# Four more portions of the second routing phase ahead of the first expert in a fused attention, routing and feed-forward kernel

## The chip, the core and the metric

One core of a Trainium2 chip runs the whole program. TensorE (PE) does matrix products, VectorE (DVE) and ScalarE (ACT) the element-wise work, GpSimd (POOL) and SyncE (SP) start transfers, POOL the gathers among them. Each engine takes its instructions in a fixed order, and they meet by semaphores. The metric is the device time of one execution in microseconds (us), lower is better; the median of several runs counts.

## What is computed

```python
def reference(**kwargs):
    attn_out = _attn_ref(...)                     # (4, 8, 576, 64): banded + downsampled attention
    x = attn_out.transpose(0, 2, 1, 3).reshape(2304, 512)
    x = _moe_ref(x=x, **moe_kwargs)               # 8 experts, each token to one of them
    return _moe2_ref(x=x, **moe2_kwargs)          # dense feed-forward 512 -> 2048 -> 512

def _moe_ref(x, w_gate, w1, w2):
    cap = N // E                                  # 2304 // 8 = 288 rows for each expert
    order = np.argsort(-(x @ w_gate).flatten())
    for idx in order:                             # greedy: the highest logit first
        tok, e = idx // E, idx % E
        if assigned[tok] >= 0 or counts[e] >= cap: continue
        assigned[tok] = e; counts[e] += 1
    for e in range(E):
        out[assigned == e] = np.maximum(x[assigned == e] @ w1[e], 0.0) @ w2[e]

def _moe2_ref(x, w_in, w_out):
    h = x @ w_in
    return (h * np.tanh(softplus(h))) @ w_out
```

## The kernel before

The program has three parts. The attention fills the first 148 us; it leaves the tokens' rows in DRAM (`x_dram`) and the gate's logits in SBUF (`L`). The routed experts run to about 440 us, and the dense feed-forward (groups A to D) after that.

**Routing.** The greedy assignment is done in eight phases; each finds the expert that fills up next and its 288 tokens. `Router.phase(k)` is a generator, and what lies between two of its `yield`s is called a portion here. A phase first makes keys and one-hot rows on DVE. Then come five levels, a search for a threshold digit by digit: DVE compares (`cmp`), PE counts with 18 small matmuls (`cnt`, one more adds the rest that is free), DVE makes a flag (`fl`), PE sums the flags (`j`), DVE reduces them (`jb`) and makes the next `E`. The tail of a phase selects tokens (`sel`), scans them (`run`), has PE place them (`pp`), compares again, and PE and DVE produce the index lists `idx` and `ii` (`it`, `rig`, `ip`) and the number of the expert, `exi`. A last portion issues three gathers of 96 rows each on POOL (`xrow`, L722). Phase 7 has no levels.

**Experts.** `FFN.expert(k, ...)` (E0 to E7) reads the expert's number into a register on SP, fetches eight pieces of weights (`wraw`, 512 KB each, L776), turns the rows over with 12 transposes on PE (`xtp`), and for each of eight `j` makes `hp` (first product), `gh` and `gl` (its two halves after the relu) and, two `j` later, 12 matmuls `ya` (second product). Weights are split by ACT (`wbh`, `wah`) and DVE (`wbl`, `wal`) into two parts. E0 and E2 use the first weights whole ("w"), the others split too ("s"). From the third piece on, E0's weights wait for the last of E0's rows. At an expert's end ACT and DVE split the results (`Yh`, `Yl`) and ACT stores them to `y_dram`.

**Pieces.** `Narrow.piece()` turns 64-bit weights of the dense part into pairs of floats: a load, one ACT operation and six DVE operations on 128 x 512 values (`nz`, `nt`), and a pair that ends it (`wM_sb`). They are put into E0, E2, E5, E6 and E7.

**Order.** `ORDER` says what is written down in which order: `R0` runs the routing until the first gather is out, `H4` four further portions, `E0/1` expert 0 with one piece. An expert has 16 steps, and with each goes one portion of the routing. What an engine's instruction stream is in the end is set by a scheduler that takes this order as priority; `add_manual_dep` with NoSync only holds an order. `busy` (L391) puts constant 128 x 512 matmuls into PE's stream (`idle`), in phase 0 and among the transposes of E0; their result isn't used.

Loads of the dense part's first operands (`Yh`, `Yl` from `y_dram`, L806) are issued early on POOL, between the gathers.

Of the kernel before, what the change touches and what calls it, by code (L numbers as in the profile page):

```python
# [56 lines left out]
class Attn:  # L57
# [175 lines left out]
    def busy(self, n):  # L233

        if not hasattr(self, 'idle'):
            self.idle = self.p_rw.tile([128, 4, 128], F32, name="idle0", tag="rw")
        for _ in range(n):
            m = self.nc.tensor.matmul(self.idle, self.a['fill'], self.a['fill'].unsqueeze(1).to_broadcast([128, 4, 128]), start=True, stop=True)
            if self.mm is not None:
                self.tc.add_manual_dep(m.ins, self.mm.ins.name, mybir.DependencyInfo(mybir.DependencyClass.NoSync, mybir.DependencyReason.DATA), reason="order")  # L240
            self.mm = m
# [95 lines left out]
class Router:  # L337
# [52 lines left out]

    def busy(self, k, n, ins):  # L391

        if k:
            return
        for _ in range(n):
            m = self.nc.tensor.matmul(self.idle.rearrange("p (r n) -> p r n", r=4), self.one, self.one.unsqueeze(1).to_broadcast([128, 4, 128]), start=True, stop=True)
            self.tc.add_manual_dep(m.ins, ins.ins.name, mybir.DependencyInfo(mybir.DependencyClass.NoSync, mybir.DependencyReason.DATA), reason="order")
            ins = m

    def behind(self, ins):  # L400

        if self.mm is not None:
            self.tc.add_manual_dep(ins.ins, self.mm.ins.name, mybir.DependencyInfo(mybir.DependencyClass.NoSync, mybir.DependencyReason.DATA), reason="order")
        return ins

    def phase(self, k):

        nc, wk, sm, L = self.nc, self.wk, self.sm, self.L
# [38 lines left out]
        if not last:  # L447
            for i in range(1, len(SH)):
                if SH[i]:
                    V.tensor_scalar(out=dg[i], in0=key, scalar1=SH[i], scalar2=KS[i] - 1, op0=ALU.arith_shift_right, op1=ALU.bitwise_and)  # L450
                else:
                    V.tensor_scalar(out=dg[i], in0=key, scalar1=KS[i] - 1, scalar2=None, op0=ALU.bitwise_and)
            yield
            for l, K in enumerate(KS):

                if l:
                    cmp = self.compare(E, K, ALU.is_ge, PARTS[k == 0])
                    yield
                end = l == len(KS) - 1
                if not end:  # L460
                    G = sm.tile([128, 18], F32, name="G")
                    V.scalar_tensor_tensor(out=G, in0=E[:, :, 0], scalar=float(KS[l + 1]), in1=dg[l + 1], op0=ALU.mult, op1=ALU.add)

                cnt = self.psr.tile([128, 8], F32, name="cnt", tag="rt")
                nr = lambda a, b: nc.tensor.matmul(cnt, self.one, self.nrem, start=a, stop=b)
                if not k:
                    nr(True, False)
                for c in range(18):
                    if not (l or k) and c == FIRST[0][1]:
                        self.busy(k, 4, ct)  # L470
                    ct = self.behind(nc.tensor.matmul(cnt, cmp[c], OH[:, c], start=(k > 0 and c == 0), stop=(k == 0 and c == 17)))
                if k:
                    nr(False, True)
                self.busy(k, 2, ct)

                fl = sm.tile([128, 8], F16, name="fl")
                V.tensor_scalar(out=fl, in0=cnt, scalar1=0.0, scalar2=None, op0=ALU.is_ge)
                yield
                j8 = self.psr.tile([128, 8], F32, name="j8", tag="rt")
                jm = nc.tensor.matmul(j8, self.sums[:, 128 * l:128 * l + 128], fl, start=True, stop=True)  # L480
                self.busy(k, 7 if end else 4, self.behind(jm))
                jb = sm.tile([128, 1], F32, name="jb")
                V.tensor_reduce(out=jb, in_=j8, op=ALU.max, axis=AX.X)
                if not end:
                    E = P2("E", BF16)
                    V.tensor_scalar(out=E, in0=two(G), scalar1=jb[:, 0:1], scalar2=-1.0, op0=ALU.subtract, op1=ALU.max)

            fw = sm.tile([128, 8], F32, name="fw")
            V.scalar_tensor_tensor(out=fw, in0=j8, scalar=jb[:, 0:1], in1=self.down, op0=ALU.is_ge, op1=ALU.mult)
            fm = sm.tile([128, 1], F32, name="fm")  # L490
            V.tensor_reduce(out=fm, in_=fw, op=ALU.max, axis=AX.X)
            ge = sm.tile([128, 2, 18], F16, name="ge")
            V.tensor_scalar(out=ge[:, 0], in0=E[:, :, 0], scalar1=jb[:, 0:1], scalar2=None, op0=ALU.is_ge)
            V.tensor_scalar(out=ge[:, 1], in0=E[:, :, 0], scalar1=jb[:, 0:1], scalar2=-1.0, op0=ALU.subtract, op1=ALU.is_equal)
        else:
            fw = sm.tile([128, 8], F32, name="fw")
            V.scalar_tensor_tensor(out=fw, in0=self.rem, scalar=30000.0, in1=self.down, op0=ALU.is_lt, op1=ALU.mult)
            fm = sm.tile([128, 1], F32, name="fm")
            V.tensor_reduce(out=fm, in_=fw, op=ALU.max, axis=AX.X)
        n = 18 if last else 36  # L500
# [9 lines left out]
        run = sm.tile([128, 36], F16, name="run")  # L510
# [8 lines left out]
        pp, cn = pc[:, 0:36], pc[:, 36:180]  # L519
        if not last:  # L520
            self.behind(nc.tensor.matmul(cn, self.one, ON.rearrange("p c e -> p (c e)"), start=True, stop=True))
        self.behind(nc.tensor.matmul(pp[:, 0:n], self.tri, s2, start=True, stop=False))
        self.busy(k, 9, nc.tensor.matmul(pp[:, 0:n], self.one, run[:, 0:n], start=False, stop=True))
        V.tensor_scalar(out=full, in0=fw, scalar1=fm[:, 0:1], scalar2=None, op0=ALU.is_equal)
        yield
        pz = sm.tile([128, 36], F32, name="pz")
# [17 lines left out]
        if not last:  # L544
            ct = sm.tile([128, 8], F32, name="ct")
# [4 lines left out]
        it = self.psr.tile([128, 4], F32, name="it", tag="rt")  # L550
        for c in range(18):
            im = self.behind(nc.tensor.matmul(it, oa[c], R[:, c], start=(c == 0), stop=(c == 17)))
        self.busy(k, 28, im)
        ig = self.igw[k % 2]
        li = ig[:, 0:3]
        V.tensor_scalar_add(li, it[0:96, 0:3], 1152.0)
# [110 lines left out]
class FFN:  # L667
# [62 lines left out]
    def expert(self, k, rows, exi):  # L730

        nc, ps = self.nc, self.ps
# [7 lines left out]
        for g in range(3):  # L740
            t = ps['h'].tile([128, 4, 96], F32, name="xtp", tag="h")
            q = slice(96 * g, 96 * g + 96)
            for dc in range(4):
                tp = nc.tensor.transpose(t[:, dc], rows[g][:, 128 * dc:128 * dc + 128], self.a['ident_sb'][0:96, 0:96])
            if g < 2:
                self.busy(k, 1 + g, tp)
            if plain:
                xc = (nc.vector.tensor_copy if g == 1 else nc.scalar.copy)(xh[:, :, q], t)
            else:
                nc.scalar.copy(xh[:, :, q], t)  # L750
                nc.vector.tensor_tensor(out=xl[:, :, q], in0=t, in1=xh[:, :, q].bitcast(F32), op=ALU.subtract)
# [117 lines left out]

ORDER = ('R0 H4 E0/1 E1 E2/2 E3 E4 E5/1 E6/2 E7/2 N A2 A4 A4 A4 A4 B4 B4 B4 B4 B2 C4 C4 C4 C4 C2 D4 D4 D4 D4 D2').split()


MAN = 0
# [33 lines left out]
def body(nc, tc, a):  # L909
    with ExitStack() as ctx:  # L910
# [39 lines left out]
        t0, ng, ns = [0] * 4, 0, 0  # L950
        for st in ORDER:
            st, *pieces = st.split('/')
# [55 lines left out]
```

## Time and profile before

| | |
|---|---|
| median of 3 runs | 851.94 us (849.99 to 852.18) |
| profiled execution | 845.38 us, span 843.6 us |
| PE busy | 812.1 us (96% of the span) |
| DVE busy | 680.3 us (81%) |
| ACT busy | 501.3 us (59%) |
| mean granted clock of TensorE | 0.994 |

The span runs from the first to the last instruction; some 1.8 us lie around it. "Busy" is the time in which an engine works on an instruction. A busy PE is not yet one at its best, since matmuls overlap: where matmuls follow each other closely, their distance counts and not their duration. The granted clock is a share of full speed: 1.00 is 2.4 GHz, 0.50 is 1.2 GHz.

### The profile page before, as it was taken

How to read it: one execution, taken by the hardware profiler on the slowest of the kernel's cores; microseconds unless marked ns; L12 is line 12 of the kernel's file. 1: busy time of each engine (PE TensorE's matmuls, PEld its weight loads, DVE VectorE, ACT ScalarE, POOL GpSimd, SP SyncE). 2: the span in 40 equal slices, each digit the busy share in tenths (PEclk: the TensorE clock that was granted, in tenths of full speed). 3: DMA queues.
4: the chain of work that ended last, by engine and by line, in shares of the span. 5: the costliest groups of instructions: out<-in, count | busy, mean ns of one | idle time of the engine just before them, and what ended most of it. 6: DMA issues, size and time to landing. Idle time of an engine off the chain costs nothing.

```text
span 843.6 us, 16899 instructions
## 1 busy us (share of the span) xinstructions
PE 812.1 (96%) x6236; PEld 685.1 (81%) x6236; DVE 680.3 (81%) x1829; ACT 501.3 (59%) x1209; POOL 175.2 (21%) x215
## 2 busy tenths in 40 slices
PE   8999999889999979899999999999999999999997
PEld 4788877458988979899998888888878888888886
DVE  6999986858889968989958788788888878657664
ACT  4787876023433434446637677777777777765552
POOL 5655320112011011021001000012223211322223
PEclk9999999999999989999999999999999999999999
DMA  8858622256467584478424444457697674973512
GB/s 217 213 169 227 195 87 96 94 178 229 141 220 248 177 269 169 144 281 276 151 97 140 128 135 148 151 160 194 145 231 173 176 194 112 246 167 118 132 51 76
DMA packets 65107, 142.41 MB, mean 169 GB/s; under 512 B 7968, under 2 KB 20640, under 8 KB 65024
## 3 DMA queue, kind: packets, MB, share of 16 engines
q1 hardware_dynamic: 24704, 70.54, 26.7%
q0 software_dynamic: 29280, 56.63, 25.9%
q10 hardware_dynamic: 11040, 14.16, 4.8%
q8 instruction: 49, 0.80, 0.4%
q14 instruction: 34, 0.28, 0.1%
HBM read 112.98 MB, written 18.88 MB: 156 GB/s over the span
## 4 chain that ended last, share of the span: by engine, by line
PE 58%; issue 6%; DMA 4%; POOL 2%; DVE 1%; ACT 1%; POOLq 0%; DVEq 0%
PE hm L704 7%; PE hm L706 7%; PE hm L705 7%; PE oa L705 6%; PE oa L706 6%; PE oa L704 6%; PE ya L704 3%; DMA xrow<-x_dram,idx 3%; PE ya L706 3%; PE ya L705 3%; PE hp L704 2%; PE hp L705 2%; PE hp L706 2%; PE hp L784 2%; DMA Yh<-y_dram 1%
## 5 line engine op out<-in xcount | busy, mean ns | idle before, releaser
L704 PE MATMUL hm<-Yh,wM_sb 128*128 128x512 f32 (+1 forms) x320 | 118.4, 370 | 1.5 <-DMA Yh<-y_dram 1.5
L706 PE MATMUL hm<-Yh,wM_sb 128*128 128x512 f32 (+1 forms) x320 | 118.7, 371 | 0.0
L705 PE MATMUL hm<-Yl,wM_sb 128*128 128x512 f32 (+1 forms) x320 | 118.6, 371 | 0.0
L704 PE MATMUL oa<-wM_sb,gh 128*128 128x512 f32 x288 | 113.1, 393 | 0.0
L705 PE MATMUL oa<-wM_sb,gh 128*128 128x512 f32 x288 | 113.1, 393 | 0.0
L706 PE MATMUL oa<-wM_sb,gl 128*128 128x512 f32 x288 | 112.9, 392 | 0.0
L858 DVE SCALAR_TENSOR_TENSOR eu<-eu 128x512 f32<-128x512 f32 x72 | 49.7, 690 | 45.0 <-ACT eu L857 44.7
L696 ACT CAST wbh<-wraw 128x512 fp32r<-128x512 f32 x64 | 39.8, 622 | 69.1 <-PE ya L705 40.4
L704 PE MATMUL ya<-gh,wbh 128*128 128x288 f32 x256 | 79.5, 314 | 0.0
L706 PE MATMUL ya<-gh,wbl 128*128 128x288 f32 x256 | 77.1, 302 | 0.0
L705 PE MATMUL ya<-gl,wbh 128*128 128x288 f32 x256 | 76.9, 301 | 0.0
L864 ACT CAST gh<-eu 128x512 fp32r<-128x512 f32 x72 | 44.3, 616 | 53.8 <-DVE eu L861 53.5
L704 PEld LDWEIGHTS hm<-Yh,wM_sb 128*128 128x128 f32 x320 | 60.2, 188 | 13.0 <-DMA Yh<-y_dram 1.9
L865 DVE TENSOR_TENSOR gl<-eu,gh 128x512 fp32r<-128x512 f32 x72 | 49.5, 688 | 24.9 <-ACT gh L864 24.4
L705 PEld LDWEIGHTS hm<-Yl,wM_sb 128*128 128x128 f32 x320 | 60.2, 188 | 11.2
L722 POOL DMA_INDIRECT xrow<-x_dram,idx x24 | 30.7, 1280 | 185.9 <-PE ip L564 95.4
L706 PEld LDWEIGHTS hm<-Yh,wM_sb 128*128 128x128 f32 x320 | 60.2, 188 | 10.7
L853 ACT ACTIVATE eu<-hm 128x512 f32<-128x512 f32 x72 | 42.9, 595 | 41.1 <-PE hm L706 40.9
L704 PEld LDWEIGHTS oa<-wM_sb,gh 128*128 128x128 f32 x288 | 54.0, 188 | 12.8 <-ACT osb L829 0.5
L855 ACT ACTIVATE eu<-eu,one_sb 128x512 f32<-128x512 f32 x72 | 52.1, 724 | 20.6 <-DVE eu L854 19.8
L706 PEld LDWEIGHTS oa<-wM_sb,gl 128*128 128x128 f32 x288 | 54.0, 188 | 12.4
L705 PEld LDWEIGHTS oa<-wM_sb,gh 128*128 128x128 f32 x288 | 54.0, 188 | 11.9
(185 smaller groups left out, 2140.8 us busy)
## 6 DMA issues: line engine op xcount, KB each, us to landing
wraw<-in_wE_dram SPq DMA_DIRECT2D x64, 512.0 KB
n<-in_wM_dram SPq DMA_DIRECT2D x32, 512.0 KB
Yh<-y_dram POOLq DMA_DIRECT2D x16, 1024.0 KB, 9.2
Yl<-y_dram POOLq DMA_DIRECT2D x16, 1024.0 KB, 7.1
part<-osb POOLq DMA_DIRECT2D x36, 256.0 KB, 4.3
vw<-in_vw_dram SPq DMA_DIRECT2D x16, 315.0 KB
kT<-in_kT_dram SPq DMA_DIRECT2D x16, 291.0 KB
qT<-in_qT_dram SPq DMA_DIRECT2D x16, 288.0 KB
```

The costliest lines, as they stand in the source:

```text
L696: c = self.nc.scalar.copy(wh, src)
L704: mm(out, lh, rh, start=first, stop=False)
L705: mm(out, lh, rl, start=False, stop=False)
L706: return mm(out, ll, rh, start=False, stop=last)
L722: ld = nc.gpsimd.indirect_dma_start(out=xr, out_offset=None, in_=self.a['x_dram'], in_offset=bass.IndirectOffsetOnAxis(ap=idx[:, g:g + 1], ...
L784: self.r.mm = nc.tensor.matmul(hp, w1[:, 128 * dc:128 * dc + 128], xh[:, dc], start=dc == 0, stop=dc == 3)
L853: nc.scalar.activation(out=e, in_=hp[:, 0:w], func=AF.Exp)
L855: nc.scalar.activation(out=u, in_=e, func=AF.Square, bias=one)
L858: nc.vector.scalar_tensor_tensor(out=u, in0=u, scalar=1.0, in1=r, op0=ALU.add, op1=ALU.mult)
L864: self.cast = nc.scalar.copy(gh[:, 0:w], e)
L865: self.mark = nc.vector.tensor_tensor(out=gl[:, 0:w], in0=e, in1=gh[:, 0:w].bitcast(F32), op=ALU.subtract)
```

## The change

`H4` becomes `H8`: four more portions of phase 1 are written down ahead of E0. The constant matmuls are dealt anew. Behind the index matmuls of phase 0 there are 14 instead of 28. The first level of phase 1 gets 3 behind its counts and 8 behind its flag sum, and E0's first transpose is held behind the last of these eight. Those among the transposes of E0 stay.

```diff
     def busy(self, k, n, ins):
 
-        if k:
+        if k > 1:
             return
         for _ in range(n):
             m = self.nc.tensor.matmul(self.idle...)
             self.tc.add_manual_dep(...)
             ins = m
+        return ins
...
                 if k:
                     nr(False, True)
-                self.busy(k, 2, ct)
+                if k == 0 or (k == 1 and l == 0):
+                    self.busy(k, 2 + k, ct)
...
                 jm = nc.tensor.matmul(j8, self.sums[:, 128 * l:128 * l + 128], fl, start=True, stop=True)
-                self.busy(k, 7 if end else 4, self.behind(jm))
+                self.behind(jm)
+                if k == 0:
+                    self.busy(k, 7 if end else 4, jm)
+                elif k == 1 and l == 0:
+                    self.ready = self.busy(k, 8, jm)
...
-        self.busy(k, 9, nc.tensor.matmul(pp[:, 0:n], self.one, run[:, 0:n], start=False, stop=True))
+        pm = nc.tensor.matmul(pp[:, 0:n], self.one, run[:, 0:n], start=False, stop=True)
+        if k == 0:
+            self.busy(k, 9, pm)
...
-        self.busy(k, 28, im)
+        if k == 0:
+            self.busy(k, 14, im)
...
                 tp = nc.tensor.transpose(t[:, dc], rows[g][:, 128 * dc:128 * dc + 128], self.a['ident_sb'][0:96, 0:96])
-            if g < 2:
+                if k == g == dc == 0:
+                    self.tc.add_manual_dep(tp.ins, self.r.ready.ins.name, ...)
+            if k == 0 and g < 2:
                 self.busy(k, 1 + g, tp)
...
-ORDER = ('R0 H4 E0/1 E1 E2/2 E3 ...').split()
+ORDER = ('R0 H8 E0/1 E1 E2/2 E3 ...').split()
```

The streams change in many places, from E0 to E7. Three of them follow. PE at the start of E0, before (`ip` is the last index matmul of phase 0, `cnt` and `j` belong to phase 1, `hp` is E0's first product; of the counts and constant matmuls only the first rows of a run are shown):

```order
L564 MATMUL ip<-ident_sb,rig_69 72x96
L744 MATMUL xtp<-ident_sb,xrow 128x96 x4
L396 MATMUL idle<-ones_66 128x512
L471 MATMUL cnt<-rOH,cmp 128x8
...
L465 MATMUL cnt<-rnrem,ones_66 128x8
L744 MATMUL xtp<-ident_sb,xrow 128x96 x4
L480 LDWEIGHTS rsum
...
L744 MATMUL xtp<-ident_sb,xrow 128x96 x4
L784 MATMUL hp<-xh,wraw 128x288 x3
```

and now:

```order
L573 MATMUL ip<-ident_sb,rig_69 72x96
L472 MATMUL cnt<-rOH,cmp 128x8
...
L482 LDWEIGHTS rsum
...
L753 MATMUL xtp<-ident_sb,xrow 128x96 x2
L472 LDWEIGHTS cmp
...
L466 MATMUL cnt<-rnrem,ones_66 128x8
L753 MATMUL xtp<-ident_sb,xrow 128x96 x2
...
L753 MATMUL xtp<-ident_sb,xrow 128x96 x4
...
L753 MATMUL xtp<-ident_sb,xrow 128x96 x4
L795 MATMUL hp<-xh,wraw 128x288
```

The counts and the flag sum of phase 1's first level have moved ahead of all transposes, those of its second level in between the first tile's four.

POOL's transfers behind the attention, before (`xrow` x6 are the gathers of two experts, `Yh` and `Yl` the early loads):

```order
L722 DMA xrow<-x_dram,idx 96x512 x6
L806 DMA Yh<-y_dram 128x4x256
L806 DMA Yl<-y_dram 128x4x256
L722 DMA xrow<-x_dram,idx 96x512 x6
L806 DMA Yh<-y_dram 128x4x512
L806 DMA Yl<-y_dram 128x4x512
L722 DMA xrow<-x_dram,idx 96x512 x12
```

and now:

```order
L731 DMA xrow<-x_dram,idx 96x512 x6
L817 DMA Yh<-y_dram 128x4x256
L731 DMA xrow<-x_dram,idx 96x512 x3
L817 DMA Yl<-y_dram 128x4x256
L731 DMA xrow<-x_dram,idx 96x512 x6
L817 DMA Yh<-y_dram 128x4x512
L817 DMA Yl<-y_dram 128x4x512
L731 DMA xrow<-x_dram,idx 96x512 x9
```

The two large loads stood ahead of the gathers of E4 and stand behind them now; one of the smaller ones stands behind the gathers of E2.

DVE at the tail of phase 6, in E5, before:

```order
L659 TENSOR_SCALAR nz<-nt 128x512
L508 SCALAR_TENSOR_TENSOR sel<-raid,fm,sel 128x18
L660 SCALAR_TENSOR_TENSOR nz<-n_4714,nz 128x512
L511 SCALAR_TENSOR_TENSOR run<-ones_66,sel 128x36
L699 TENSOR_TENSOR wbl<-wraw,wbh 128x512
L661 TENSOR_TENSOR nt<-nt,nz 128x512
L794 SCALAR_TENSOR_TENSOR gl<-hp,gh 128x288
```

and now:

```order
L513 SCALAR_TENSOR_TENSOR sel<-own,fm,ge 128x36
L532 TENSOR_SCALAR full<-fw,fm 128x8
L514 SCALAR_TENSOR_TENSOR sel<-raid,fm,sel 128x18
L805 SCALAR_TENSOR_TENSOR gl<-hp,gh 128x288
L517 SCALAR_TENSOR_TENSOR run<-ones_66,sel 128x36
```

The piece's operations have left this tail; they stand further on in the stream, between the `ii` of phase 6 and the `run` of phase 7.

## Rows read from the trace of the kernel before

**Rows 1.** Waits of PE: line, what for, us in total, times, longest

```profile
PE xtp L744 <- DMA xrow<-x_dram,idx: 6.0, 3, 4.9
PE cnt L471 <- DVE cmp L388: 3.2, 8, 1.3
```

**Rows 2.** Windows E0, E1, E2, E4, E5, E6: busy by engine, clock, DMA, GB/s

```profile
175.00:208.00 33.00, 29.84 (x257) 24.57 (x257) 24.30 (x92) 10.30 (x20) 4.68 (x3) 1.00 0.65 232
208.00:241.00 33.00, 32.63 (x354) 31.23 (x352) 28.15 (x104) 13.86 (x29) 5.28 (x5) 1.00 0.63 189
241.00:275.00 34.00, 32.97 (x286) 28.06 (x284) 30.05 (x107) 13.16 (x27) 3.44 (x3) 1.00 0.63 210
307.00:346.00 39.00, 34.05 (x349) 32.80 (x346) 28.88 (x104) 15.17 (x32) 3.01 (x3) 0.91 0.56 173
346.00:377.00 31.00, 28.78 (x251) 27.65 (x251) 28.23 (x104) 14.36 (x31) 4.46 (x3) 0.94 0.58 197
...
390.00:400.00 10.00, 10.00 (x78) 10.00 (x76) 9.89 (x20) 5.88 (x13) 0.00 (x0) 1.00 0.97 327
```

**Rows 3.** The same view, of the stretches behind the holes of E4 and E5

```profile
312.90:318.00 5.10, 5.07 (x36) 4.90 (x37) 1.78 (x4) 1.49 (x4) 0.00 (x0) 0.56 0.02 6
358.30:362.00 3.70, 3.67 (x15) 3.61 (x16) 3.70 (x18) 0.00 (x0) 0.00 (x0) 0.54 0.83 280
```

**Rows 4.** Timeline of PE, start of E4: start, us, instruction [idle before <-releaser]

```profile
312.93 0.90 PE L744 MATMUL xtp<-ident_sb,xrow 96*128 96x96 f32 x4 [4.95 <-DMA xrow<-x_dram,idx]
```

**Rows 5.** Timeline of POOL, 222 to 300 us

```profile
223.79 0.82 POOL L806 DMA_DIRECT2D Yh<-y_dram  x1 [19.27 <-PE j L480]
...
231.62 1.15 POOL L722 DMA_INDIRECT xrow<-x_dram,idx  x1 [5.84 <-PE hp L706]
...
290.87 0.80 POOL L806 DMA_DIRECT2D Yh<-y_dram  x1 [21.45 <-DMA y_dram<-Yl]
...
296.05 1.28 POOL L722 DMA_INDIRECT xrow<-x_dram,idx  x1 [2.82 <-PE ip L564]
```

**Rows 6.** The view of the tile xrow, all gathers

```profile
DMA to landing us min/median/max: 3.0/6.2/16.8
```

**Rows 7.** Timeline of PE, end of phase 0 and start of E0

```profile
165.11 6.20 PE L396 MATMUL idle<-ones 128*128 128x512 f16 x28
...
173.91 0.55 PE L744 MATMUL xtp<-ident_sb,xrow 96*128 96x96 f32 x4
175.03 1.72 PE L784 MATMUL hp<-xh,wraw 128*128 128x288 f32 x6 [0.57 <-ACT xh L748]
...
179.22 0.17 PE L480 MATMUL j<-fl,rsum 128*128 128x8 f16 x1 [1.41 <-DVE fl L477]
...
183.33 0.60 PE L471 MATMUL cnt<-rOH,cmp 128*128 128x8 f16 x18 [1.35 <-DVE cmp L388]
```

**Rows 8.** Timelines of DVE and ACT in the same stretch

```profile
166.64 1.34 DVE L388 TENSOR_TENSOR cmp<-E,rthr 128x2304 f16<-128x2304 bf16 x1
...
177.75 0.62 ACT L696 CAST wbh<-wraw 128x512 fp32r<-128x512 f32 x1 [2.77 <-DMA wraw<-in_wE_dram]
...
178.40 0.69 DVE L699 TENSOR_TENSOR wbl<-wraw,wbh 128x512 fp32r<-128x512 f32 x1 [2.63 <-ACT wbh L696]
...
180.41 0.62 ACT L696 CAST wbh<-wraw 128x512 fp32r<-128x512 f32 x1 [2.05 <-DMA wraw<-in_wE_dram]
```

**Rows 9.** Timeline of DVE in E5, the tail of phase 6

```profile
355.40 0.42 DVE L659 TENSOR_SCALAR nz<-nt 128x512 int32<-128x512 int32 x1
355.74 0.23 DVE L508 SCALAR_TENSOR_TENSOR sel<-raid,fm,sel 128x18 f16<-128x18 f32 x1
355.89 0.69 DVE L660 SCALAR_TENSOR_TENSOR nz<-n,nz 128x512 f32<-128x512 uint32 x1
356.49 0.23 DVE L511 TENSOR_TENSOR_SCAN run<-ones,sel 128x36 f16<-128x36 f16 x1
...
358.32 1.54 DVE L767 TENSOR_TENSOR Yl<-ya,Yh 128x288 fp32r<-128x288 f32 x4
```

More of the change, by code (lines that the diff above doesn't have):

```diff
@@ L744, in expert @@
                 tp = nc.tensor.transpose(t[:, dc], rows[g][:, 128 * dc:128 * dc + 128], self.a['ident_sb'][0:96, 0:96])
-            if g < 2:
+                if k == g == dc == 0:
+                    self.tc.add_manual_dep(tp.ins, self.r.ready.ins.name, mybir.DependencyInfo(mybir.DependencyClass.NoSync, mybir.DependencyReason.DATA), reason="order")
+            if k == 0 and g < 2:
                 self.busy(k, 1 + g, tp)
@@ L868, in group @@
             yield
-ORDER = ('R0 H4 E0/1 E1 E2/2 E3 E4 E5/1 E6/2 E7/2 N A2 A4 A4 A4 A4 B4 B4 B4 B4 B2 C4 C4 C4 C4 C2 D4 D4 D4 D4 D2').split()
+ORDER = ('R0 H8 E0/1 E1 E2/2 E3 E4 E5/1 E6/2 E7/2 N A2 A4 A4 A4 A4 B4 B4 B4 B4 B2 C4 C4 C4 C4 C2 D4 D4 D4 D4 D2').split()
 MAN = 0
```

## The prediction

> **What bounds the kernel now.** The waits of TensorE (PE) come first [rows 1]. In the middle of the program, where the experts run, its waits are few: 6.0 us for gathered rows (4.9 of it once) and 3.2 us for compares of the routing. The second view cuts the experts' part into their stretches [rows 2]: PE is busy 32.63 of 33 us in E1 and 32.97 of 34 in E2, so a gain can only come from the holes, and these are 3.16 us in E0 (33.00 - 29.84), 0.37 in E1, 1.03 in E2, 4.95 in E4 and 2.22 in E5. VectorE (DVE) is busy 24 to 30 us of the same stretches: it isn't the bound, but it has little room. The third view is the clock [rows 3]: behind the holes of E4 and E5 TensorE was granted 0.56 and 0.54 of full speed, that is mostly its lower level (1.2 GHz), over 5.10 and 3.70 us. That costs 5.10 x 0.44 = 2.24 us and 3.70 x 0.46 = 1.70 us more. E4's hole is therefore worth 4.95 + 2.24 = 7.2 us, E5's 2.22 + 1.70 = 3.9 us. After E0's holes of 1.41 and 1.35 us the clock stayed at 1.00 [rows 2].
>
> Whose fault is E4's hole? Its first transpose waits 4.95 us for rows, until 312.93 [rows 4]. The gather was issued at 296.05, behind the two loads of Yh and Yl (1 MB each) that stand from 290.87 on in the same queue [rows 5]. Gathers take 6.2 us to land in the median and 16.8 at most [rows 6]; 312.93 - 296.05 is 16.9, so 16.8 is this one, the first rows being asked for 12 us before they were needed.
>
> **The change part by part.** The sum is made against the profiled execution: 845.38 us, of which 843.6 are its span. The median of the runs shown is 851.94, so I carry differences over.
>
> 1. *Four portions earlier, E4.* Every routing phase now stands four portions further ahead of its expert. One portion goes with each of an expert's 16 steps, and an expert takes 31 to 34 us [rows 2]: by steps that is some 8 us. Read from the order it is less: of the hundred or so DVE rows between the last xl of E3 and the first of E4, the cast that makes the indices of phase 4 is the 60th before and the 41st now, a fifth of some 32 us, so about 6 us. The gather of E4 then goes out at about 290, and in POOL's queue the two 1 MB loads now stand behind it, not ahead. It is needed at 308. Even with the worst landing of the trace (16.8) it would be 307, with the median one 296. I take the whole hole as gone: -7.2 us. The bounds are -7.2 and 0 (rows as late as before).
>
>  What stands behind POOL's new order: the gather of E2 is now queued behind the load of Yh that waits for E0's output (223.79 [rows 5]). The gather would be ready about 6 us before 231.62, at 225.6, so POOL is free again in time; this costs nothing, and if E0's output came 10 us later, E2 would still have its rows. The loads of Yh and Yl that go back are wanted only after E7.
>
>  The Trainium skill, "DMA: Bandwidth & Descriptors", section "Queues, rings and completion order", says that each engine takes the descriptors of one ring in order and goes round-robin between queues. By that rule rows queued behind 2 MB in their own queue come late whatever the other queues do; the trace's 16.8 us agrees. It would put the sum at the same -7.2.
>
> 2. *E2 and E1.* E2's first transposes wait 1.03 us for rows [rows 2]; these were asked for at 231.62 [rows 5] and are now asked for 6 us earlier: -1.0 (bounds -1.0 and 0). The small holes about the start of E1 (0.40 of E0's 3.16 after its two big ones, and 0.37) hang on E1's weights, whose fetch needs the expert's number from the same phase: -0.7 (bounds -0.7 and 0).
>
> 3. *The start of E0.* This is what the change pays. PE's queue now holds the first level and half of the second of phase 1 in front of and among the transposes. The 28 constant matmuls took 6.20 us from 165.11 [rows 7], 0.22 each; 14 end at 168.2. The compare of the first level ends at 167.98 [rows 8], so its 18 counts follow with no wait, to 169.2. DVE has then two splits, a flag, a reduction, a new E and the second level's compare of 1.34 us [rows 8] to do, and is through at about 172.3. PE fills 1.7 of it with 8 constant matmuls; then two transposes, the counts of level two (0.6 us), two transposes, the four of the second tile, the four of the third. The third tile's transposes, which started at 173.91 when their rows had come, now start at about 174.4, and the first matmul of E0, at 175.03 [rows 7], at about 175.5: +0.5. Bounds 0 (rows later than 174.4 anyway) and +1.2 (a second compare's length late).
>
>  Then E0's two holes. Before, a flag of the routing stood in DVE behind a split of weights that landed at 177.75 (cast 177.75, split 178.40 [rows 8]); PE stood 1.41 us in front of the flag's matmul at 179.22, and 1.35 us at 183.33 for a compare held by the weights of 180.41 [rows 7, 8]. The new order of DVE has the same pattern one level on: the flag of level three behind the split of 178.40, the compare of level four behind the split of the weights of 180.41. PE reaches them at 177.8 and 181.0 and is let go at 179.3 and 182.6: 1.5 + 1.6 = 3.1 us against 2.76, +0.3. The weights themselves come no earlier, since their fetch waits for the last of the first rows as before. Together E0 costs +0.8; bounds 0 and +2.
>
>  A rule speaks against this part: the Trainium skill, "TensorE: Matmul & The Clock Gate", section "What happens when you issue a matmul", says that matmuls stay in program order and only weight loads are pulled ahead. The row at 179.22 agrees: ready matmuls stood 1.41 us behind the routing's. If the transposes could pass, the +0.5 would be 0 and the sum 8.2 instead of 7.7.
>
> 4. *E5.* Here PE waited for the tail of phase 6 while DVE worked on a piece of the later weights (nz, nt): 0.42 and 0.69 us between a selection and the run that PE needed [rows 9]. The tail of phase 6 is now free of pieces. But the piece has gone into the tail of phase 7: from the cast of ii to the run of phase 7 the new order of DVE has six such operations (3 x 0.34 + 3 x 0.60 start to start, as 355.40 to 355.74 and 355.89 to 356.49 show [rows 9]), three Yl (1.54 / 4 = 0.38 each [rows 9]) and small ones, 4.9 us, while PE has 21 matmuls of 0.13 us (10.00 / 78 [rows 2]), 2.8 us. So PE stands for about 2.5 us at that run, against 2.22: the hole moves, and I take the clock's loss to come with it, +0.4. Bounds -3.9 (gone) and +1.
>
> 5. *The constant matmuls.* 28 become 14, and 11 come in with phase 1's first level: 3 fewer of 0.22 us, all while the rows are on their way. Nothing, as long as PE has no long gap there; the longest in the new order is under 1 us.
>
> Sum: -7.2 - 1.0 - 0.7 + 0.8 + 0.4 = -7.7 us. 845.38 becomes 837.7, and the median 851.94 - 7.7 = **844.2 us**.
>
> **The rivals.** (a) E5's hole goes too, since DVE runs ahead of where the walk has it: -3.9 - 0.4 more, 839.9. For it: DVE gains some room when E4's hole no longer bunches its work. Against: 2.8 us of PE work against 4.9 us of DVE work. (b) E4's rows still come late, because the weights of E4, asked for earlier too, crowd the same engines: half the wait and the whole loss of clock stay, 2.5 + 2.2 = 4.7, 848.9. Against it: 12 us of margin by the median landing. (c) A new hole of E5's size opens where the routing now meets other DVE work, +3.9: 848.1. DVE at 30.05 of 34 us in E2 [rows 2], whose two pieces now meet the tail of phase 3, speaks for it; that PE has more matmuls between the marks there than in E5 speaks against it. (d) Slower: in E0 the two holes now lie 1.7 us apart instead of 2.7, and TensorE falls to its lower level there. From 177.8 to some 200 every matmul would take twice its time, half of 22 us: +11, 855.2. It decides from where the two holes act like one: the trace has full clock after 1.41 and 1.35 us lying 2.7 us apart, and the lower one after E5's hole, which is shorter than their sum. (e) The portions don't pay: phase 1 hangs on E0's weights, so the later phases gain only a few us and E4's rows stay where they are; only the small terms remain, 850.5.
>
> **How the numbers follow.** Chances: the forecast 0.52 (its own range 842 to 846.5), (a) 0.13, (b) 0.10, (c) 0.12, (d) 0.07, (e) 0.06. A measurement of this kernel can tell about 0.3% from no change, 2.6 us. Faster by more: the forecast, (a), half of (b) and most of (c), 0.80. Within: the rest of (b) and (c), and (e), 0.13. Slower: (d), 0.07. The range for 8 in 10 takes in (b) and (c) and most of (a): 839 to 850.
>
> **What would show it.** In the trace after: no wait of E4's first transpose over 1 us and full clock behind it; the gather of E4 issued about 290 and ahead of the 1 MB loads; E0's first matmul at about 175.5, with two holes of some 1.5 us; E5 with a hole of 2 to 3 us at the run of phase 7 and the lower clock behind it. The prediction is wrong in its main step if the rows of E4 are late again, and wrong in its pay-back if E0 loses more than 2 us or its clock.

## The result: 837.5 us where 844.2 were forecast

| us | before | changed |
|---|---|---|
| median, first comparison (19 executions each) | 851.94 | 837.52 |
| ratio, with its 95% interval | | 0.983 (0.980 to 0.985) |
| ratio in three later comparisons | | 0.987 (0.982 to 0.992), 0.983 (0.979 to 0.987), 0.988 (0.985 to 0.991) |
| median of the executions whose clock is on record (61 and 33) | 850.67 | 837.52 |
| median granted clock of these | 0.988 | 0.996 |
| median of time x granted clock | 840.4 | 833.2 |

The sign was right and the gain nearly twice as large as forecast: 13 to 14 us instead of 7.7, below the low end of the range (839). The last two lines of the table split it: about 7 us are waits, and about 6 us are clock. (Time x clock counts the lower clock also where PE waits anyway, so it is a rough split.) The ratios and the last three lines leave out the few slow executions, which run some 1.5% or more above the fastest at a lower clock.

The profile recorded with the result is of an execution that ran with the lower clock for some 24 us in the attention; the rows below are from another execution of the same kernel (new8_again). Its page has PE busy 97% of a span of 835.4 us:

```profile
span 835.4 us, 16916 instructions
PE 808.7 (97%) x6233; PEld 682.7 (82%) x6233; DVE 679.6 (81%) x1829; ACT 500.7 (60%) x1209; POOL 175.9 (21%) x215
```

The waits of PE, which answer to [rows 1] (line, what for, us in total, times, longest). The wait for rows that headed that list is gone altogether; those for compares, flags and Yl are left:

```profile
PE cnt L472 <- DVE cmp L388: 2.7, 7, 1.1
PE j L482 <- DVE fl L479: 1.6, 2, 1.4
...
PE ya L713 <- DVE Yl L778: 1.2, 2, 1.0
...
PE cnt L472 <- DVE ii L575: 0.9, 1, 0.9
```

The stretches of E0, E1, E2, E4 and E5, which answer to [rows 2] (us, busy time of each engine with its instructions, granted clock, DMA share, GB/s):

```profile
177.00:212.00 35.00, 32.30 (x296) 26.32 (x296) 25.75 (x98) 10.51 (x20) 4.41 (x3) 0.95 0.68 225
212.00:241.00 29.00, 28.96 (x298) 27.82 (x296) 25.20 (x93) 12.66 (x27) 5.47 (x5) 1.00 0.70 213
241.00:277.00 36.00, 36.00 (x315) 31.38 (x313) 33.57 (x115) 14.28 (x30) 2.77 (x3) 1.00 0.65 221
308.00:340.00 32.00, 32.00 (x351) 30.86 (x350) 29.37 (x106) 15.42 (x32) 3.81 (x3) 1.00 0.63 206
340.00:372.00 32.00, 29.91 (x268) 28.24 (x267) 30.31 (x107) 15.63 (x33) 8.51 (x6) 1.00 0.63 209
```

E1, E2 and E4 have no hole at all. E0 has 2.7 us and now a clock of 0.95; E5 has 2.1 us, with full clock.

POOL's timeline, which answers to [rows 5]: the gathers of E4 are asked for at 290.88, and the two loads go out behind them.

```profile
290.88 1.83 POOL L731 DMA_INDIRECT xrow<-x_dram,idx  x1 [28.75 <-PE ip L573]
293.02 0.91 POOL L731 DMA_INDIRECT xrow<-x_dram,idx  x1 [0.30 <-issue]
294.23 1.15 POOL L731 DMA_INDIRECT xrow<-x_dram,idx  x1 [0.30 <-issue]
296.35 0.80 POOL L817 DMA_DIRECT2D Yh<-y_dram  x1 [0.97 <-DMA y_dram<-Yh]
```

And PE at the start of E4, which answers to [rows 4]; seven transposes run with no wait in front of them:

```profile
307.94 0.74 PE L753 MATMUL xtp<-ident_sb,xrow 96*128 96x96 f32 x7
```

**Where the time went, by stage.** The stretches below are cut at the first transposes of the experts in PE's timeline. They begin at the cast of the first list of indices (`idx` of phase 0, in DVE's timeline), since all streams are the same in both kernels up to the end of phase 0, and end at the first `hm`, where the dense part begins. "Five" is the mean over five profiled executions of each kernel.

| us | before, first profile | before, five | changed, five | difference of the fives | forecast |
|---|---|---|---|---|---|
| idx to E1 (with E0) | 43.41 | 42.92 | 45.24 | +2.3 | +0.8 |
| E1 and E2 | 66.69 | 69.11 | 64.52 | -4.6 | -1.7 |
| E3 and E4 | 70.02 | 70.51 | 62.99 | -7.5 | -7.2 |
| E5 | 34.28 | 34.27 | 32.55 | -1.7 | +0.4 |
| E6 and E7 | 56.63 | 56.64 | 56.51 | -0.1 | 0 |
| sum | 271.03 | 273.46 | 261.82 | -11.6 | -7.7 |

The sum lay between 271.0 and 276.9 us in the five executions of before, and between 259.0 and 264.7 in those of the changed kernel; the dense part took 406.5 to 407.2 us in all ten. So 11.6 of the 13 to 14 us are where they were looked for, and three of the terms had the wrong size, one of them the wrong sign.

### The profile page after: what moved, and what is told of

Same layout as the page of the kernel before. It is cut to its first block, busy times and chain, and to the rows that moved or that the text cites. A ratio compares the mean times of both kernels' runs of the same rounds, so it can differ in the third digit from the quotient of the medians.

```text
span 844.8 us, 16916 instructions
## 1 busy us (share of the span) xinstructions
PE 816.6 (97%) x6233; PEld 688.6 (82%) x6233; DVE 681.0 (81%) x1829; ACT 500.9 (59%) x1209; POOL 175.7 (21%) x215
## 3 DMA queue, kind: packets, MB, share of 16 engines
q0 software_dynamic: 29280, 56.63, 26.1%
## 4 chain that ended last, share of the span: by engine, by line
PE 75%; DVE 9%; issue 6%; DMA 5%; POOL 2%; ACT 2%; SPq 0%; POOLq 0%; ACTq 0%; DVEq 0%
PE hm L713 7%; PE hm L715 7%; PE hm L714 7%; PE oa L714 6%; PE oa L715 6%; PE oa L713 6%; PE ya L714 4%; PE ya L715 4%; PE ya L713 4%; PE hp L713 3%; PE hp L795 3%; PE hp L714 3%; PE hp L715 3%; PE cnt L472 2%; PE pvl L223 2%
## 5 line engine op out<-in xcount | busy, mean ns | idle before, releaser
L713 PEld LDWEIGHTS hm<-Yh,wM_sb 128*128 128x128 f32 x320 | 60.3, 188 | 13.2 <-DMA Yh<-y_dram 2.1
L714 PEld LDWEIGHTS oa<-wM_sb,gh 128*128 128x128 f32 x288 | 54.1, 188 | 11.9
```

Source lines behind the costliest of these rows:

```text
L713: mm(out, lh, rh, start=first, stop=False)
L714: mm(out, lh, rl, start=False, stop=False)
```

## The experiments

**The kernel before again** (no edit), for a second profile:

> The kernel before, unchanged, so that its median of 851.94 us has a second profile beside the one of 845.38 us. Theory 1: the 6.6 us between the two lie in the routed experts: in most runs the rows of E4 come still later than in the run first profiled, so a new profile near the median shows a wait of E4's first transpose of 8 to 12 us instead of 4.95, and the lower clock behind it for longer than 5 us. Theory 2: they lie in the attention or in the dense part (clock, loads), and E4's wait is again 4 to 6 us; the changed kernel then gets its additional 6 us from there. Time by both: 849 to 853 us.

849.91 us, and a profile at 849.55. E4's transposes wait 3.37 us (theory 1 had 8 to 12), but E1's wait for rows too, which they did not in the first profile, and the lower clock follows. Neither theory was quite it. Three further profiles of the same kernel followed, to see which of its holes cost clock, and one of the changed kernel:

> A further profile of the kernel before, for how often each of its holes costs clock. Theory (the first profile was one of the best executions, since fewer of its holes drew the lower clock): E4's wait for rows of 3 to 5 us and its loss of 2.5 to 3.4 us of clock are in each of these looks; E1's wait for rows, 1.5 us or more, with 1.7 us of clock, in most of them, and E5's loss of 1.7 us in some; together 5 to 9 us of clock lost between the routing and the dense part. Rival (the executions differ in the attention): the experts lose about 5 us in each, and the attention 0 to 5.

> The same kernel and the same expectation as the look before it.

> The same kernel and the same expectation as the two looks before it.

> A further profile of the changed kernel. Theory: no wait for rows in any expert, 0 to 3.4 us of clock lost in E0 and none in E1 to E7. Rival: E0 loses 3.4 us or more each time that its two holes lie close, and the stretch from the first index cast to the dense part's first matmul is 264 us or more.

The changed kernel had had a second profile before that:

> The changed kernel, unchanged, for a profile without the low clock in the attention (21 to 63 us) that its first profile has. 836 to 838 us; from the casting of the first indices to the first transpose of E7 222 us as in the first profile (231 in the kernel before), E4 without a wait for rows, and a clock of 1.00 through all experts.

The three further executions of the kernel before: 851.84, 851.61 and 849.62 us. The changed kernel: 839.86 us (median, ratio 0.987) and 835.62. In the profile of the first of these E0 takes 41.48 us from its first transpose to E1's and draws the lower clock, so that it is 234.8 us from the cast to E7's first transpose; the first profiles of the two kernels have 241.1 and 232.1 (the 231 and 222 us of the expectation are each 10 us too low). The second takes 261.93 us from the cast to the dense part. In the second of the three further profiles (b_look2) PE's timeline has waits for rows at the starts of E1, E2 and E4 (start, us, instruction, idle before and its releaser), and the pair of waits in E5:

```profile
211.00 0.55 PE L744 MATMUL xtp<-ident_sb,xrow 96*128 96x96 f32 x4 [1.14 <-DMA xrow<-x_dram,idx]
212.05 0.90 PE L744 MATMUL xtp<-ident_sb,xrow 96*128 96x96 f32 x4 [0.50 <-DMA xrow<-x_dram,idx]
...
245.91 0.84 PE L744 MATMUL xtp<-ident_sb,xrow 96*128 96x96 f32 x4 [0.72 <-DMA xrow<-x_dram,idx]
...
316.38 0.55 PE L744 MATMUL xtp<-ident_sb,xrow 96*128 96x96 f32 x4 [3.45 <-DMA xrow<-x_dram,idx]
...
362.80 0.18 PE L523 MATMUL pp<-run,ones 128*128 128x36 f16 x1 [0.57 <-DVE run L511]
364.36 0.41 PE L704 MATMUL hp<-xh,wah 128*128 128x288 f32 x1 [1.38 <-DVE gl L794]
```

Behind each of them the clock fell, as the windows of 5 us of the same execution show (granted clock third from the right):

```profile
210.00:215.00 5.00, 3.50 (x18) 3.31 (x19) 3.04 (x7) 1.33 (x3) 0.00 (x0) 0.69 0.04 10
...
245.00:250.00 5.00, 4.28 (x18) 3.50 (x17) 3.11 (x8) 0.48 (x1) 0.00 (x0) 0.66 0.46 172
315.00:320.00 5.00, 2.67 (x15) 2.19 (x16) 1.81 (x4) 1.42 (x3) 0.00 (x0) 0.77 0.17 48
320.00:325.00 5.00, 5.00 (x41) 4.85 (x40) 1.41 (x4) 1.03 (x3) 0.00 (x0) 0.55 0.02 3
365.00:370.00 5.00, 5.00 (x27) 5.00 (x28) 4.44 (x20) 0.62 (x1) 0.00 (x0) 0.66 0.57 211
```

5 x (1 - 0.69) = 1.6 us, 1.7, then 1.2 + 2.3, then 1.7. Summed over windows of 5 us from the routing to the dense part, the kernel before loses 5.1, 5.2, 6.9, 8.5 and 5.1 us of clock in its five executions, the changed one 0, 1.7, 0, 1.7 and 1.7. E4's hole draws the lower clock in five of five executions, E5's pair of waits in four, E1's rows in two, E2's in one. The attention loses 0, 3.4, 5.2, 1.7 and 3.4 us besides: the first profile is the only one of the five without a loss there. The theory of these runs holds in its main part (the experts lose 5 to 8.5), but E1's clock fell in two of the four and not in most, and the attention has a share, which the change doesn't touch.

**The two loads behind E4's gathers, in the kernel before** (all other engines keep their order):

```diff
-            if k == 0:
-                self.g0 = ld
+            if k in (0, 4):
+                setattr(self, f'g{k}', ld)
...
-            nc.gpsimd.dma_start(t, self.a['y_dram'][...])
+            yl = nc.gpsimd.dma_start(t, self.a['y_dram'][...]); ng = t0 == 2 and part == 0 and self.tc.add_manual_dep(yl.ins, self.g4.ins.name, ...)
```

> The kernel before, with one edit: the two 1 MB loads of Yh and Yl that stand ahead of E4's gathers in POOL's order stand behind them. PE, DVE, ACT and SP keep their order. Theory 1 (most of the change is E4's rows, and the typical run loses more there than the profiled one): 851.9 - 7 to 13, so 839 to 845 us, E4's first transpose with no wait over 1 us and full clock behind it. Theory 2 (the typical run loses elsewhere): no more than the 7.2 us of the profile, 844.5 to 846 us. Rival (the rows are late because of the weights that are under way, not because of these two loads): 850 to 852 us, the wait stays.

841.99 us, ratio 0.989 (0.985 to 0.993). The gathers of E4 are asked for no earlier than before, at 299.54, and the loads follow them:

```profile
299.54 0.91 POOL L722 DMA_INDIRECT xrow<-x_dram,idx  x1 [26.49 <-PE ip L564]
...
303.63 0.83 POOL L806 DMA_DIRECT2D Yh<-y_dram  x1
```

PE's timeline of the same execution, at the start of E4:

```profile
311.81 1.19 PE L744 MATMUL xtp<-ident_sb,xrow 96*128 96x96 f32 x12
```

Twelve transposes run in a row with no wait, 12.3 us after the rows were asked for; behind the loads the same rows took 16.9 us in the first profile and 15.8 in b_look2 (316.38 - 300.58). The stretch of E3 and E4 is 63.99 us, against 70.51: that is 6.5 of the 7.5 us that the change takes off it. The weights that were under way are the same, so the rival falls: the loads ahead in the queue made the rows late. E1's wait for rows is still there in this run (1.60 and 0.66 us, and a clock of 0.77), as nothing was done for it.

**Six portions, constant matmuls as before** (`R0 H6` in the kernel before):

> Six portions ahead of E0, the constant matmuls as before the change. In POOL's order E4's gathers stand behind the 1 MB loads as before the change, but are asked for some 4 us earlier. Theory (E4's rows are late for the loads ahead of them in the queue): a wait for E4's rows of up to 2 us is left, and E1's rows come with less or no wait; 840 to 846 us. If only the time of asking counts and not the place in the queue: no wait in E4, 837 to 840. If only the place counts: the whole wait of 3 to 5 us is there, 845 to 849.

840.19 us, ratio 0.989 (0.985 to 0.993). E4 has no wait. Its gathers stand behind one of the two loads, not behind both as was expected, and are asked for at 290.36, 15.3 us before they are needed (POOL's timeline, then PE's at the start of E4):

```profile
288.21 0.79 POOL L806 DMA_DIRECT2D Yh<-y_dram  x1 [22.78 <-issue]
290.36 1.21 POOL L722 DMA_INDIRECT xrow<-x_dram,idx  x1 [1.35 <-DVE ii L566]
...
294.81 0.82 POOL L806 DMA_DIRECT2D Yl<-y_dram  x1
```

```profile
305.68 0.25 PE L744 MATMUL xtp<-ident_sb,xrow 96*128 96x96 f32 x1
```

How long the three gathers of E4 take from asking to landing goes with what stands ahead of them (the view of the tile `xrow` over these three gathers, first before the change with both loads ahead, then here with one, then in the changed kernel with none):

```profile
DMA to landing us min/median/max: 14.8/16.0/16.8
DMA to landing us min/median/max: 11.2/12.1/12.2
DMA to landing us min/median/max: 6.9/7.1/7.6
```

So each of the two loads ahead goes with some 4 to 5 us. Two remedies were enough: no load ahead with 12.3 us of time, or one load ahead with 15.3. Since six portions moved one load back as well, no run shows what asking earlier is worth with both loads still ahead. The changed kernel has 17.1 us (from 290.88 to 307.94) and no load ahead, which is more margin than needed. E5's hole is not helped by six portions: 1.89 us in one piece, and 3.4 us of clock.

**The dealing alone** (the changed kernel with `R0 H4`), **and the portions alone** (the kernel before with `R0 H8`), the latter three times and twice beside the changed kernel:

> The changed kernel with four portions ahead of E0 instead of eight: the new dealing of the constant matmuls alone. By the prediction it is worth nothing: 850.5 to 853.5 us, with E4's rows late as before (the 1 MB loads stand ahead of its gathers again). If the dealing is itself a part of the gain, it comes out at 846 us or less, E0 starting 2 to 3 us earlier, as 14 constant matmuls of 0.22 us are gone there.

> The kernel before with eight portions ahead of E0 instead of four and nothing else: the portions alone, the constant matmuls as before (28 behind the index matmuls, none with phase 1's first level). By the prediction the dealing is worth nothing, so 837 to 840 us, as the changed kernel. If the dealing pays for the earlier portions' cost, it is slower than the changed kernel: 28 constant matmuls of 0.22 us ahead of phase 1's counts hold these by 3 us, the first product comes 2 to 3 us later, 840 to 843 us.

> Eight portions ahead of E0 with the constant matmuls as before the change, a second time and beside the changed kernel, in five rounds. Theory (the new dealing has a price in E0: its first two holes and sometimes the clock): the stretch from the first index cast to the dense part's first matmul is 259 to 261 us against 262 to 265 with the new dealing, and the median 1 to 4 us below the changed kernel's. Rival (the two profiles differed by chance): the medians agree within 1 us and the stretches overlap.

> The changed kernel beside the one with the dealing as before: 836 to 840 us, E0 39 to 41.5 us from its first transpose to E1's; by the rival of the run above 37 to 38.

> Eight portions with the constant matmuls dealt as before the change. Theory (the new dealing costs E0 some 3 us, as four profiles of the changed kernel beside two of this one have it): E1's first transpose 41 to 43 us after the first index cast, the median 2 to 4 us below the changed kernel's of the same job. Rival (the price is made up for elsewhere, or the profiles were chance): the median within 1.5 us of the changed kernel's, or above it as in the last pair.

> The changed kernel beside it. Theory: E1's first transpose 45 to 48 us after the first index cast, 836 to 840 us. Rival: 42 to 43 us, as in one profile of five.

The dealing alone: 852.75 us, ratio 1.002 (0.999 to 1.005), no gain. The portions alone: 839.74, 838.59 and 838.18 us, with the changed kernel at 835.24 and 838.73 beside the last two. Taken together the medians are 838.28 (15 executions) and 837.52 (33). In the profiles the dealing isn't free: E1's first transpose comes 42.80, 41.35 and 43.11 us after the first index cast with the old dealing and 45.55, 47.70, 42.54, 45.45 and 44.98 with the new one. Of these 2.8 us in the mean, 1.0 is clock: it fell in E0 in three of the five with the new dealing and in none of the three with the old. The profile of the dealing alone has it too (a wait of 3.25 us for a compare, 3.4 us of clock, E1's first transpose after 45.51 us). The times do not show the 2.8 us: the pairs differ by 3.4 us for the new dealing and by 0.6 against it. Where they come back isn't settled, the theory that the new dealing makes the kernel slower is borne out by neither pair, and "the dealing is worth nothing" stands within some 3 us.

**E0's weights earlier** (the dependence "rows first" on the first gather instead of the last, in the changed kernel):

```diff
-            if k == 0:
+            if k == 0 and g == 0:
                 self.g0 = ld
```

> The changed kernel, with E0's weights from the third piece on waiting for the first of E0's three gathers instead of the last. It measures E0's pay-back. Theory (E0's holes of 1.1 to 2.6 us are the routing's flag and compare standing in DVE behind a split whose weights land late): the third piece lands 1.5 to 3 us earlier, the holes shrink by as much each, E0 gets 2.5 to 4 us shorter, and the clock stays at 1.00 in it; 834 to 837 us beside 838 to 840 for the changed kernel. Rival (the weights only change places with the rows): the third tile's transposes wait 1.5 to 2.5 us for rows instead, the first product starts that much later, and the time stays within 1 us of the changed kernel's.

838.40 us, ratio 0.985 (0.977 to 0.994): no gain to be seen. The rival is right. The two holes are gone, and the third tile's rows are late instead, with the lower clock behind it (PE's timeline, then the window):

```profile
175.16 0.90 PE L753 MATMUL xtp<-ident_sb,xrow 96*128 96x96 f32 x4 [1.84 <-DMA xrow<-x_dram,idx]
```

```profile
175.00:180.00 5.00, 4.27 (x29) 3.08 (x30) 1.80 (x4) 2.23 (x4) 0.00 (x0) 0.50 1.03 406
```

Rows and weights share the same 406 GB/s there (DMA share 1.03): this order of the transfers moves the price of E0's start and doesn't remove it.

The same profile shows what a lower clock costs in E5, where this run has the instruction order of the changed kernel. The clock fell there behind the first wait for `Yl` (PE's timeline, then the windows):

```profile
352.08 0.40 PE L713 MATMUL ya<-gh,wbh 128*128 128x288 f32 x1 [0.99 <-DVE Yl L778]
```

```profile
350.00:355.00 5.00, 4.01 (x22) 3.71 (x21) 4.92 (x22) 0.01 (x1) 2.79 (x2) 0.75 1.01 364
355.00:360.00 5.00, 5.00 (x36) 4.87 (x36) 5.00 (x16) 2.07 (x4) 1.10 (x1) 0.91 1.02 329
```

That is 1.7 us of clock lost, and yet E5 took the same 32.55 us as in all five profiles of the changed kernel: the three waits that follow in those (0.20, 0.52 and 0.18 us for DVE) are gone here. PE, slower, only came later to what it would else have waited for.

**E5's piece moved to E3** (`E3/1 E4 E5` in the changed kernel):

> The changed kernel with the piece of E5 moved to E3. Prediction's step 4 says the piece costs a hole of 2.5 us and 1.7 us of clock in E5 at the run of phase 7; the profile of the changed kernel shows 0.52 us there, and 0.99 at the Yl of E5's results. If these two come from the piece, E5 gets 1 to 1.5 us shorter and E3, which gets the piece, no more than 0.5 longer; within 1 us of the changed kernel's time, 836 to 840. If the piece makes a hole in E3 as it did in E5 of the kernel before, E3 grows by 2 to 4 us: 839 to 843.

837.39 us, ratio 0.981 (0.974 to 0.989). E5 gets 2.4 us shorter (30.13 us), E3 and E4 1.2 and 1.1 longer (32.43 and 32.87): the sum of the three is the same to 0.1 us. E5 gains and E3 pays more than expected, and the piece's DVE work costs about as much in either place.

**Twelve portions**, with the new dealing and the old:

> The changed kernel with twelve portions ahead of E0. Theory (the gain is the margin of the gathered rows, and with eight portions no expert waits for rows any more): four more bring nothing to the rows and hold E0 by the levels that then stand ahead of its first products, 1 to 4 us: 838 to 843 us. Rival (each four portions are worth several us in themselves): 830 to 834.

> Twelve portions ahead of E0, the constant matmuls as before the change. In POOL's order the gathers stand as with eight. Theory (with eight no expert waits for rows, so that more margin is worth nothing): within 2 us of the run with eight portions and the same dealing, with E0 longer by what the four portions' compares and counts hold it, up to 2 us. Rival (the twelve portions of the earlier run were quicker than the eight because the routing's tail then lies in E0 and its holes are passed sooner): 1 to 3 us faster than with eight.

836.99 us, ratio 0.980 (0.970 to 0.989), and 839.56, ratio 0.989 (0.985 to 0.993): no better than eight. With the old dealing E4 has a new hole: its `xl`, which PE needs, stands on DVE behind the keys and the compare of a phase's first portion, and the clock falls once more (PE's timeline, then the window).

```profile
317.03 0.61 PE L704 MATMUL hp<-xh,wah 128*128 128x288 f32 x1 [2.80 <-DVE xl L751]
```

```profile
315.00:320.00 5.00, 2.97 (x11) 2.79 (x12) 4.58 (x13) 0.00 (x0) 2.72 (x3) 0.60 0.75 231
```

That is what rival (c) of the prediction described; it didn't come with eight portions and came with twelve. None of these versions is faster than the changed kernel by more than the runs can tell.

## Why the prediction came out as it did

**Which step failed: "I carry differences over".** The forecast missed by 6.7 us (844.2 - 837.5). Set against the one profile that it was made from, the sum is off by only 1.5 us: the stretches go from 271.0 to 261.8, -9.2 where -7.7 was forecast. The other 5.2 us aren't in that profile: 2.4 us that the five executions of the kernel before lose more than it in the same stretches (273.46 - 271.03, as much as E1 and E2 alone differ by), and 2.8 us by which the medians of the first comparison differ beyond the stretches (14.4 against 11.6), of which the cause is open. That the 837.7 us which the sum gave for the profiled execution lies beside the measured median is chance.

**E4, step 1: right, in place and size.** The gather went out at 290.88, "about 290" as read from the order, ahead of the loads, and the hole is gone with its clock: -7.5 us against -7.2. The experiment with the two loads alone gives 6.5 of it from this one cause. The Trainium skill's rule that was set beside it ("DMA: Bandwidth & Descriptors", section "Queues, rings and completion order": one ring's descriptors are taken in order) agrees with the loads' run: same weights under way, rows in 12.3 us or less instead of 16.9. There the Trainium skill says it of the rings that SP and ACT fill; that POOL's queue behaves so is shown by these rows.

**E1 and E2, step 2: mechanism right, size wrong; this is the term with the largest error.** -1.7 was read from one execution in which E1's rows happened to be in time; [rows 1 and 2] show no wait for them. In the four others E1's second or third transposes wait 0.75 to 1.9 us for rows, and in two of them the clock falls behind it. The changed kernel has those rows in time in all five: asked for 4.6 us earlier after the index cast (195.88 - 167.34 against 199.58 - 166.46) and needed 2.3 us later. These are POOL's first gather of E1 and, before it, DVE's first index cast, in b_look2 and in new8_again:

```profile
199.58 0.91 POOL L722 DMA_INDIRECT xrow<-x_dram,idx  x1 [27.36 <-DVE idx L559]
195.88 2.44 POOL L731 DMA_INDIRECT xrow<-x_dram,idx  x1 [22.63 <-DVE dg L434]
```

```profile
166.46 0.16 DVE L559 CAST idx<-rig 96x3 int32<-96x3 f32 x1
167.34 0.16 DVE L568 CAST idx<-rig 96x3 int32<-96x3 f32 x1
```

Against the first profile alone the term is -2.2, against five -4.6. Either this error of 2.9 us or that of 2.1 in E5 below is enough to put 837.5 under the range, whose low end is 839.

The profiled execution of 845.38 us was 6.6 us below its median, and the prediction named that gap and went past it. It should have been a question: what do most executions lose that this one didn't? Its granted clock was 0.994, and the median of 61 executions is 0.988, 5 us more of lower clock. A change that takes holes away takes the losses behind them too, and they aren't all in the one trace.

**E0, step 3: too small.** The first product starts 9.5 us after the index cast instead of 9.05 (means of the five), +0.4 where +0.5 was forecast. The rows of PE (answering to [rows 7]):

```profile
170.66 0.59 PE L472 MATMUL cnt<-rOH,cmp 128*128 128x8 f16 x18 [0.90 <-DVE ii L575]
...
176.71 0.75 PE L795 MATMUL hp<-xh,wraw 128*128 128x288 f32 x2 [0.57 <-ACT xh L759]
...
180.39 0.17 PE L482 MATMUL j<-fl,rsum 128*128 128x8 f16 x1 [1.40 <-DVE fl L479]
...
183.26 0.61 PE L472 MATMUL cnt<-rOH,cmp 128*128 128x8 f16 x18 [1.15 <-DVE cmp L388]
```

One step of the walk was wrong without harm: the counts did wait, 0.90 us, for `ii`, a cast that frees the one PSUM buffer which `ip` and `cnt` share and that stands in DVE behind a split of weights. The two holes came one level on, as forecast: 1.40 and 1.15 us here, 1.10 and 2.55, 1.83 and 1.79, 1.44 and 0.21, 1.26 and 0.62 in the others. In the mean that is 2.7 us together, as before, and not the 3.1 of the walk. What the sum left out is the clock: it fell behind them in three of five executions, 1.7 us each (in this one to 0.68 over 185 to 190 us), 1.0 in the mean. Rival (d) had that, at +11. Start and clock make 1.4 of the +2.3 that was measured instead of +0.8; the rest is not assigned to a row.

**E5, step 4: the work right, its effect wrong.** The step's own figures, 4.9 us of DVE's work and 2.8 of PE's, make a wait of 2.1 us and not 2.5, and so -0.1 instead of +0.4. DVE does take longer than PE from the cast of `ii` to phase 7's run. But PE does not stand once for 2.5 us; it meets the same lateness in four pieces:

```profile
353.59 0.40 PE L713 MATMUL ya<-gh,wbh 128*128 128x288 f32 x1 [0.99 <-DVE Yl L778]
...
355.90 0.40 PE L713 MATMUL ya<-gh,wbh 128*128 128x288 f32 x1 [0.20 <-DVE Yl L778]
...
357.83 0.17 PE L529 MATMUL pp<-run,ones 128*128 128x18 f16 x1 [0.52 <-DVE run L517]
358.18 0.40 PE L714 MATMUL ya<-gl,wbh 128*128 128x288 f32 x1 [0.18 <-DVE gl L805]
```

Together 1.89 us, nearly as much as the pair of before (0.57 + 1.38 = 1.95), and yet the clock stays at 1.00:

```profile
350.00:355.00 5.00, 3.84 (x41) 3.31 (x41) 4.74 (x21) 1.49 (x3) 1.49 (x2) 1.00 0.98 331
355.00:360.00 5.00, 4.07 (x28) 3.36 (x27) 5.00 (x14) 1.14 (x2) 2.41 (x2) 1.00 0.98 329
```

The failed half-sentence is "I take the clock's loss to come with it". The walk looked only at the run and missed that the `ya` of the next accumulation wait for the `Yl` that empty their buffers first. The clock's price was wrong too. In the kernel before, E5 took 32.97 us in the one execution without the lower clock, and 34.1 to 34.5 with 1.7 us of it lost; in the changed order 1.7 us lost cost nothing in the one execution that shows it (E0's weights earlier). So, as far as single executions show it, some 1.3 of the -1.7 us measured hang on the lower clock and 0.4 on the work; why the divided wait drew it in none of five is not shown.

**The constant matmuls, step 5: right** within the 3 us that the runs tell, with E0's stretch in the profiles left open as said above.

**The rivals.** Rival (a) came in part: E5 lost its lower clock and kept its waits, -1.7 of -3.9. Rival (d) came at 1.7 us in three of five executions. Rivals (b), (c) and (e) did not come with eight portions. The 850.5 us of rival (e) does not follow from the prediction's small terms: -1.0 - 0.7 + 0.8 + 0.4 make -0.5, so 851.4.

**What stays open.** The stretches differ by 11.6 us, the medians by 13.2 over the 61 and 33 executions and 14.4 in the first comparison. The attention lost 0 to 5.2 us of clock in the profiles of before and 0 to 1.7 in four of the changed kernel's (11.9 in the fifth), with the same instructions in the same order; five executions don't settle whether that is chance.

## What to carry to other kernels

Before a forecast is made against a profile, set that execution's time and granted clock beside the other runs: if it is one of the best, the holes that a change removes cost more in most runs than in this trace. Read a gather's safety as its margin, from the row that asks for it to the row that needs it, and ask what stands ahead of it in its queue: here 12 us with two large loads ahead was late every time, and 12 us without them or 15 with one was not. Before a lower clock is counted as a loss, ask whether TensorE would have waited for another engine anyway: in E5 of the changed order 1.7 us of it cost nothing.

## What was not expected of the hardware

Whether a hole draws the lower clock is not fixed by its length: 1.38 + 0.57 us of waiting in E5 drew it in four of five executions, and 0.99 + 0.20 + 0.52 + 0.18 us, in the same place, in none of five. Nor does the division of the wait alone settle it: in the run with E0's weights earlier, with E5's order unchanged, the clock fell behind the 0.99 us. Waits for rows of 0.75 to 1.9 us at E1's start drew it in two of four. Where it fell, the loss came in two sizes, 1.6 to 1.7 us (E1, E2, E0 of the changed kernel, three of E5's four) and 3.4 to 3.5 us (E4, and the fourth of E5), counted over windows of 5 us and so with the part that fell into the wait itself.
